# Ten of sixteen weight loads issued from ScalarE's queue in place of SyncE's, in an attention and mixture-of-experts kernel

## The chip, the cores and the metric

The kernel runs on one core of a Trainium2 chip. The metric is the device time of one execution in microseconds; the kernel before took 539.23 us (median of three runs, 539.05 to 540.62). The names of the engines are those of the profile: PE (matmul, with PEld for its weight loads), DVE (vector engine), ACT (scalar engine), POOL, and SP, which only issues transfers. ACT can issue transfers too, on a queue of its own.

## The reference

Attention that keeps the 32 largest scores of each row, followed by a dense mixture of four experts:

```python
scores = scale * np.matmul(q, k.transpose(0, 1, 3, 2))      # 2 x 8 heads, 576 x 576, head dim 64
kth = np.partition(scores, -top_k, axis=-1)[..., -top_k:-top_k + 1]      # top_k = 32
scores = np.where(scores >= kth, scores, -1000000000.0)
attn = np.exp(scores - np.max(scores, axis=-1, keepdims=True))
attn = attn / (np.sum(attn, axis=-1, keepdims=True) + 1e-09)
x = np.matmul(attn, v)                                       # -> 1152 x 512
...
p = domain_probs / (domain_probs.sum(-1, keepdims=True) + 1e-09)
for e in range(E):                                           # 4 experts, 512 -> 1024 -> 512
    h = np.maximum(x @ w1[e], 0.0)
    out += p[:, e:e + 1] * (h @ w2[e])
```

## The kernel before

The 1152 rows are cut into ten tiles: for each of two batches four of 128 rows and one of 64. The first tile worked on is the 64-row tile of batch 0. A tile is cut into units, one for each head (four units of two heads for a 64-row tile); they are numbered u = 0, 1, 2, ... through the whole program. For one unit PE computes the scores (`emit_qk`, L643), DVE finds the 32 largest by four rounds of MAX8 and three of MATCH_REPLACE8 (`topk_op`, L656 to L660), ACT takes the exponential (`emit_exp`, L700), DVE or ACT and POOL apply the mask (L707 to L717), ACT and POOL split the result into two fp16 halves (`emit_a`, L725 to L729), a DMA transposes it (`emit_at`, L735, issued by SP), and PE multiplies it by v (`emit_av`, L765). When all heads of a tile are done, the experts run on it: `m1` (L882 to L884), `h_hi` and `h_lo`, `m2` (L929), `evac`.

The expert weights are eight matrices, named by (e, j): expert e, j = 0 for w1 and j = 1 for w2. Each is loaded in two halves of 1 MB (`load_w`, L342; halves a = 0 and a = 2), so there are sixteen loads. Each matrix then goes through four steps. `w_gram` (L498) is 32 matmuls on PE that run over the raw matrix: the first 16 read the half a = 0, the last 16 the half a = 2. `w_diag` (L504 on DVE, L507 on PE) and `w_total` (L280, L282 on DVE) make a scale out of that. `w_raw` (L527, ACT) scales the raw matrix, and `w_split` (L533 on ACT, L536 on POOL) cuts it into fp16 halves, the form that the experts use. The order in which the matrices are taken is (0,0), (1,0), (0,1), (1,1), (2,0), (3,0), (2,1), (3,1). The two matrices of expert 3 take the place of a scratch area that the first tile uses, so their loads wait until that is free.

Every step is a function registered with `at`. A table `ISSUE` gives each step its place in one global order, and each engine executes its instructions strictly in that order: an instruction that waits holds up all that stands behind it on its engine. The transfers of SP and ACT, in the global order, use eight completion semaphores in turn, so an issue also waits until the eighth transfer before it has landed.

In the global order the ten loads that the change touches stand at these places on ACT's side: both halves of (1,0) between two L1086 instructions at about 21.7 us of the trace; the first half of (0,1) between an L533 and an L700 at 31.1; its second half between an L1101 and an L573 at 34.1; both halves of (1,1) between an L700 and an L527 at 36.2; both halves of (2,0) between an L533 and an L700 at 56.4; half a = 2 of (2,1) between an L533 and an L700 at 62.0; half a = 0 of (2,1) between an L533 and the first L893 at 66.3. On PE the `w_gram` of (2,0) stands between the scores of unit 7 and those of unit 8; behind it follow the first `m1` and the scores of units 9 and 10.

Of the kernel before, what the change touches and what calls it, by code (L numbers as in the profile page):

```python
# [229 lines left out]
def attn_moe_kernel(tc, q, k, v, probs, w1, w2, out):  # L230
    nc = tc.nc
    PE, ACT, DVE, POOL, SP = nc.tensor, nc.scalar, nc.vector, nc.gpsimd, nc.sync
# [29 lines left out]
    def at(place, fn, *args):  # L262

        i = len(known)
        known.append(fn.__name__)
        heapq.heappush(events, (ISSUE[i][0] if ISSUE else place, i, 0, fn, args))
# [20 lines left out]
    with tc.manual_schedule(engines={getattr(mybir.EngineType, x) for x in MANUAL}):  # L287
# [202 lines left out]
        def w_scale(e, j, place):  # L490
            st = {}

            def w_gram():
                st["g"] = g = bank(ps_m1, "m1")
                hi16 = wt[e, j].rearrange("p c f -> p (c f)").bitcast(BF16)
                hi16 = hi16.rearrange("p (n t) -> p n t", t=2)[:, :, 1]
                for c in range(32):
                    PE.matmul(g[:, 0:128], lhsT=hi16[:, c * 128:(c + 1) * 128], rhs=hi16[:, c * 128:(c + 1) * 128],  # L498
                              start=(c == 0), stop=(c == 31))

            def w_diag():
                g = st["g"]
                dg = stp.tile([128, 1], F32, tag="gd", name="gd")
                DVE.scalar_tensor_tensor(g[:, 0:128], g[:, 0:128], 1.0, ident, op0=OP.mult, op1=OP.mult, accum_out=dg)  # L504
                yield
                st["pt"] = g[:, 256:257]
                PE.matmul(st["pt"], lhsT=ones, rhs=dg, start=True, stop=True)  # L507

            def w_total():
                s = ws[:, e, j:j + 1]  # L510
                wscale[e, j] = s
                yield from pow2(st, st["pt"], C_W2 if j else C_W1, 1, "w", dst=s, inv=iw[:, e, j:j + 1])
                if (e, j) == (WORDER[-1], 1):
                    yield 1
                    DVE.tensor_tensor(iwp, iw[:, :, 0], iw[:, :, 1], op=OP.mult)
                    yield 1
                    iwb = iwp.rearrange("p (g e) -> p g e", g=1).to_broadcast([128, 5, E])
                    DVE.tensor_tensor(pniw[:, 0:5], pn[:, 0:5], iwb, op=OP.mult)

            at(place, w_gram)  # L520
            at(place + P["diag"], w_diag)
            at(place + P["wtot"], w_total)
# [604 lines left out]
        swap = 10 * last_of[tiles[0]] + P["av_first"] + 1  # L1127
# [70 lines left out]
        for m, (e, j) in enumerate(worder):  # L1198
            for a in (0, 2):
                n = 4 * m + a  # L1200
                x = P["w_load"] + P["w_load_pace"] * (n - P["w_early"])
                if n < P["w_early"]:
                    x = P["w_first"] if n < 3 else P["w_second"]
                at(max(x, swap + 0.1) if e == 3 else x, load_w, SP, e, j, a, a + 2)
            g = P["gram"][m]
            w_scale(e, j, g)
            g = max(P["split"][m], g + P["diag"], raw_used.get((e, j), 0) + 0.1)
            for i in range(2):
                at(g + 2 * P["wsplit_pace"] * i - 0.1, w_raw, e, j, i)
            for i in range(4):  # L1210
                at(g + P["wsplit_pace"] * i, w_split, e, j, i, W_MODE[4 * m + i])

        while events:
            place, i, n, f, args = heapq.heappop(events)
# [38 lines left out]
```

## Time and profile before

| | |
|---|---|
| median of three runs | 539.23 us |
| the profiled execution | 540.16 us, of which the span of the trace is 538.4 us |
| PE busy, whole span | 505.1 us (94%) |
| DVE busy | 433.7 us (81%) |
| ACT busy | 365.0 us (68%) |
| POOL busy | 361.4 us (67%) |

The span falls into two parts. Up to about 118 us the weights are loaded and prepared and the first tiles pass through attention; after that PE works nearly without a break. Busy shares of the whole span mix the two parts, so engines are read by stretches. "Idle before" behind an instruction tells how long its engine stood still before it and what released it. The DMA-issuing instructions of SP and ACT appear as SPq and ACTq.

### The profile page before, as it was taken

Reading aid. Unit: us, or ns where it says so; the run is one execution under the profiler, and the core shown is the slowest. Engines: PE = TensorE matmul, PEld = TensorE weight load, DVE = VectorE, ACT = ScalarE, POOL = GpSimd, SP = SyncE. Lnnn points to the kernel's source line nnn. Section 1 sums busy time; section 2 is a strip of 40 time slices with the busy share of each in tenths; the row PEclk is TensorE's granted clock in tenths of the full one; section 3 lists DMA queues with packets and bytes.
Section 4 is the critical chain, followed back from the end, with each engine's and each line's share of the span. In section 5 each row is a group of like instructions: output and inputs, shape, how many; then the busy total and the mean of one; then the engine's idle time right before and its main releaser. Section 6 shows DMA issues by size and latency. Waiting matters only on the chain.

```text
span 538.4 us, 16332 instructions
## 1 busy us (share of the span) xinstructions
PE 505.1 (94%) x6738; PEld 384.6 (71%) x6738; DVE 433.7 (81%) x969; ACT 365.0 (68%) x602; POOL 361.4 (67%) x397
## 2 busy tenths in 40 slices
PE   7887758699999999999999999999999999999996
PEld 5666644586778677777777678677777778667766
DVE  3999997999999999999999989999999686610101
ACT  2999997998777777897768666764656635442121
POOL 0499997999877677978967866574665754253211
PEclk9997798799999999999999999999999999999999
DMA  8999998552474277574553642452423322214001
GB/s 218 311 255 331 265 280 170 104 90 47 99 144 75 65 111 128 94 139 93 122 113 88 110 70 66 83 89 45 76 52 62 71 45 47 43 24 65 12 2 32
DMA packets 142779, 58.37 MB, mean 108 GB/s; under 512 B 130096, under 2 KB 134448, under 8 KB 142704
## 3 DMA queue, kind: packets, MB, share of 16 engines
q1 hardware_dynamic: 139280, 54.50, 49.9%
q10 hardware_dynamic: 3424, 2.82, 1.7%
q8 instruction: 53, 0.87, 0.7%
q14 instruction: 22, 0.18, 0.1%
HBM read 25.45 MB, written 2.36 MB: 52 GB/s over the span
## 4 chain that ended last, share of the span: by engine, by line
PE 78%; DVE 14%; DMA 2%; ACT 2%; SPq 2%; issue 1%; POOL 0%; DVEq 0%
PE m L929 34%; PE m L882 11%; PE m L883 11%; PE m L884 11%; DVE m L656 6%; PE av L765 5%; PE ps L643 5%; DVE w L660 3%; DVE w L658 2%; DVE w L707 2%; DMA at<-a 2%; DMA pn<-in_moe_domain_probs_dram 1%; ACT w L533 1%; ACT w L527 1%; PE m L940 1%
## 5 line engine op out<-in xcount | busy, mean ns | idle before, releaser
L884 PE MATMUL m<-xt,w 128*128 128x128 f16 (+1 forms) x1280 | 199.8, 215 | 0.1
L929 PE MATMUL m<-w,h 128*128 128x512 f16 (+1 forms) x912 | 191.4, 383 | 0.0
L882 PE MATMUL m<-xt,w 128*128 128x128 f16 (+1 forms) x1120 | 178.9, 215 | 0.0
L883 PE MATMUL m<-xt,w 128*128 128x128 f16 (+1 forms) x1120 | 178.8, 215 | 0.0
L656 DVE MAX8 m<-w 128x8 f32<-128x576 f32 x216 | 161.6, 754 | 3.2
L929 PEld LDWEIGHTS <-h 128*128 128x128 f16 (+1 forms) x912 | 81.6, 101 | 88.4 <-issue 2.2
L884 PEld LDWEIGHTS <-w 128*128 128x128 f16 x1280 | 124.0, 99 | 0.2 <-POOL w L536 0.2
L882 PEld LDWEIGHTS <-w 128*128 128x128 f16 x1120 | 108.8, 99 | 2.6 <-issue 1.0
L907 POOL TENSOR_TENSOR h<-hf,h 128x512 f16<-128x512 f32 x59 | 68.4, 1160 | 62.6 <-ACT hf L900 62.2
L883 PEld LDWEIGHTS <-w 128*128 128x128 f16 x1120 | 108.5, 99 | 1.6
L660 DVE MATCH_REPLACE8 w<-m,w 128x576 f32<-128x576 f32 x144 | 106.9, 742 | 0.0
L727 POOL TENSOR_TENSOR a<-w,a 128x512 f16<-128x512 f32 x68 | 78.9, 1161 | 32.9 <-ACT a L725 17.9
L700 ACT ACTIVATE w<-ps,nb,es 128x576 f32<-128x576 f32 x68 | 56.3, 829 | 52.3 <-DVE m L656 46.1
L717 POOL TENSOR_TENSOR w<-w,d 128x576 f32<-128x576 f32 x48 | 61.4, 1282 | 27.6 <-ACT d L714 27.5
L893 ACT ACTIVATE h<-m 128x512 f16<-128x512 f32 x72 | 42.4, 593 | 53.5 <-PE m L884 35.9
L656 DVE MAX8 m<-ps 128x8 f32<-128x576 f32 x72 | 54.3, 755 | 15.2 <-PE ps L599 8.2
L725 ACT ACTIVATE a<-w 128x576 f16<-128x576 f32 x68 | 45.9, 679 | 13.2 <-POOL w L717 12.0
L658 DVE MATCH_REPLACE8 w<-m,ps 128x576 f32<-128x576 f32 x72 | 53.8, 747 | 0.0
L643 PE MATMUL ps<-kt,qa 128*128 128x288 f16 x128 | 34.9, 292 | 10.9 <-DVE w L707 10.0
L765 PEld LDWEIGHTS <-at 128*128 128x128 f16 (+1 forms) x1008 | 36.9, 101 | 9.1 <-DMA at<-a 3.5
L765 PE MATMUL av<-vt,at 128*128 128x65 f16 (+1 forms) x1008 | 39.4, 196 | 3.2 <-DMA at<-a 3.2
L900 ACT ACTIVATE hf<-m 128x512 f32<-128x512 f32 x59 | 34.9, 591 | 7.5 <-POOL h L907 6.0
(166 smaller groups left out, 759.1 us busy)
## 6 DMA issues: line engine op xcount, KB each, us to landing
w<-in_moe_w_dram SPq DMA_DIRECT2D x16, 1024.0 KB, 8.1
qraw<-in_q_dram SPq DMA_DIRECT2D x8, 256.0 KB, 3.4
qb<-qa SPq DMA_DIRECT2D x16, 128.0 KB, 2.6
out_dram<-o ACTq DMA_DIRECT2D x8, 256.0 KB, 2.2
at<-a SPq DMA_TRANSPOSE x68, 3.3
vraw<-in_v_dram SPq DMA_DIRECT2D x2, 512.0 KB, 7.4
nraw<-in_v_dram SPq DMA_DIRECT2D x4, 256.0 KB, 2.9
kraw<-in_k_dram SPq DMA_DIRECT2D x4, 256.0 KB, 2.9
```

The costliest lines, as they stand in the source:

```text
L643: PE.matmul(ps[:, 0:288], lhsT=src[:, x, :], rhs=kt[x].rearrange("p c n -> p (c n)")[:, ks], start=(j == 0), stop=(j == 1))
L656: DVE.max(m, s_t[u] if r == 0 else w_t[u])
L658: DVE.match_replace(rows2(w_t[u]), m, s_t[u], NEG)
L660: DVE.match_replace(w_t[u], m, w_t[u], NEG)
L717: POOL.tensor_tensor(w, w, g, op=OP.mult)
L727: POOL.tensor_tensor(a[:, 640:1152], w[:, 0:512], a[:, 0:512], op=OP.subtract)
L765: PE.matmul(o, lhsT=att[:, blk, ps], rhs=r, start=(i == 0), stop=(i == len(seq) - 1))
L882: PE.matmul(o, lhsT=HI[e, 0, c][:, fc], rhs=xs(0, c), start=(c == 0), stop=False)
L883: PE.matmul(o, lhsT=HI[e, 0, c][:, fc], rhs=xs(1, c), start=False, stop=False)
L884: PE.matmul(o, lhsT=LO[e, 0, c][:, fc], rhs=xs(0, c), start=False, stop=(c == 3))
L907: POOL.tensor_tensor(h[:, 1], hf, h[:, 0], op=OP.subtract)
L929: PE.matmul(y[z * 64:z * 64 + M, :], lhsT=h_t[es, qd][:, p // 2, h0:h0 + M], rhs=w, start=(fc == 0 and p == 0), stop=(fc == 7 and p == 2))
```

## The change

One line of the loop that places the weight loads. Every load was issued by SP; now the two halves of (0,0) and the four halves of expert 3's matrices stay with SP, and all others go to ACT. That is ten loads by the condition in the code (a short description of the change speaks of eight). The places in the global order are the same. The data that each load moves, the tile that it fills and the steps that read it are unchanged.

```diff
--- before.py
+++ after.py
@@ -1201,7 +1201,7 @@
                 x = P["w_load"] + P["w_load_pace"] * (n - P["w_early"])
                 if n < P["w_early"]:
                     x = P["w_first"] if n < 3 else P["w_second"]
-                at(max(x, swap + 0.1) if e == 3 else x, load_w, SP, e, j, a, a + 2)
+                at(max(x, swap + 0.1) if e == 3 else x, load_w, SP if e == 3 or n < 4 else ACT, e, j, a, a + 2)
             g = P["gram"][m]
             w_scale(e, j, g)
             g = max(P["split"][m], g + P["diag"], raw_used.get((e, j), 0) + 0.1)
```

Here `n` is 4 times the place of the matrix in the order above plus the half `a`, so `n < 4` is the matrix (0,0).

## Rows read from the trace of the kernel before

**Rows 1.** Stretches: from, to, length, busy us of PE, PEld, DVE, ACT, POOL; clock.
```profile
10.00:118.00 108.00, 81.92 (x1242) 67.61 (x1241) 103.59 (x269) 100.11 (x126) 92.09 (x68) 0.89 0.97 232
20.00:56.00 36.00, 27.02 (x357) 22.24 (x355) 35.83 (x94) 35.74 (x45) 31.42 (x22) 0.91 1.16 288
118.00:538.00 420.00, 416.14 (x5459) 312.25 (x5455) 329.29 (x698) 262.27 (x472) 268.30 (x316) 1.00 0.40 75
```

**Rows 2.** Timeline of SP: start, duration us, line, transfer, count.
```profile
31.70 4.84 SPq L342 DMA_DIRECT2D w<-in_moe_w_dram  x3
...
43.77 0.58 SPq L342 DMA_DIRECT2D w<-in_moe_w_dram  x1
...
48.82 1.75 SPq L342 DMA_DIRECT2D w<-in_moe_w_dram  x1
...
63.04 3.04 SPq L342 DMA_DIRECT2D w<-in_moe_w_dram  x3
```

**Rows 3.** Timeline of ACT, at the places named above.
```profile
35.42 0.74 ACT L700 ACTIVATE w<-ps,nb 128x576 f32<-128x576 f32 x1
...
55.46 1.05 ACT L533 ACTIVATE w<-w 128x1024 f16<-128x1024 f32 x1
56.41 0.82 ACT L700 ACTIVATE w<-ps,nb,es 128x576 f32<-128x576 f32 x1
...
66.32 0.58 ACT L893 ACTIVATE h<-m 128x512 f16<-128x512 f32 x1
```

**Rows 4.** Timeline of ACT around one store that ACT issues (ACTq).
```profile
428.64 0.58 ACT L893 ACTIVATE h<-m 128x512 f16<-128x512 f32 x1
428.66 0.34 ACTq L983 DMA_DIRECT2D out_dram<-o  x1
429.12 0.59 ACT L900 ACTIVATE hf<-m 128x512 f32<-128x512 f32 x1
```

**Rows 5.** Weight loads by window: issue ns min/median/max and starts; us to landing.
```profile
L342 SPq DMA_DIRECT2D w<-in_moe_w_dram x2: 583/1167/1751, 43.8 to 48.8; - x2
DMA to landing us min/median/max: 6.7/7.4/8.2
...
L342 SPq DMA_DIRECT2D w<-in_moe_w_dram x3: 601/725/1623, 63.0 to 64.5; - x3
DMA to landing us min/median/max: 8.3/10.2/12.0
...
L342 SPq DMA_DIRECT2D w<-in_moe_w_dram x14: 367/594/2176, 16.7 to 83.3; - x14
```

**Rows 6.** Waits of SP: who waited, for whom, us in total, times, longest.
```profile
SPq L328 <- DMA w<-in_moe_w_dram: 0.4, 1, 0.4
```

**Rows 7.** Timeline of PE.
```profile
52.31 1.08 PE L498 MATMUL m<-w 128*128 128x128 bf16 x16
57.02 1.89 PE L498 MATMUL m<-w 128*128 128x128 bf16 x16 [3.64 <-DMA w<-in_moe_w_dram]
...
70.85 0.30 PE L643 MATMUL ps<-kt,qa 128*128 128x288 f16 x1 [2.60 <-DVE w L707]
...
76.31 0.28 PE L643 MATMUL ps<-kt,qb 128*128 128x288 f16 x1
79.81 0.76 PE L765 MATMUL av<-vt,at 128*128 128x65 f16 x14 [3.21 <-DMA at<-a]
...
85.33 0.36 PE L507 MATMUL m<-gd,ones 128*128 128x1 f32 x2
```

**Rows 8.** Timeline of DVE.
```profile
60.17 0.75 DVE L656 MAX8 m<-ps 128x8 f32<-128x576 f32 x1
...
81.38 0.79 DVE L707 SCALAR_TENSOR_TENSOR w<-ps,m,w 128x576 f32<-128x576 f32 x1
85.72 0.16 DVE L280 TENSOR_SCALAR wpt<-m 128x1 int32<-128x1 int32 x1 [3.55 <-PE m L507]
```

**Rows 9.** The chain of work that ended last, in order of time.
```profile
71.40 8.36 DMA at<-a
```

## The prediction

> **What bounds the kernel now.** I read the stretches first. From 10 to 118 us DVE is busy 103.59 of 108.00 us, ACT 100.11, PE only 81.92; from 118 us to the end PE is busy 416.14 of 420.00 [rows 1]. So the second part is a fixed amount of PE work in a fixed order: whatever delays PE at 118 us delays the end by as much, and nothing there gives it back. The first part is DVE's, and DVE stands still there for 4.4 us in all. That is the most that any change of the loads can win. Of this, 3.55 us is one wait, at 85.72, for a small PE matmul [rows 8]. PE came late to that matmul because it had stood still for 3.21 us until 79.81 for a transposed tile [rows 7], whose DMA took 8.36 us from 71.40 on [rows 9].
>
> The next view is the timeline of PE at the weight loads. The `w_gram` of (2,0) reads its first half at 52.31, then PE waits 3.64 us for the second half and goes on at 57.02 [rows 7]. That half was issued by SP at 48.82 [rows 2] and landed 8.2 us later [rows 5]. So this load is already the one that PE waits for; its first half was issued at 43.77 [rows 2]. In PE's order the scores of unit 8 stand behind it, and DVE takes them up at 60.17 [rows 8], 3.15 us after PE went on.
>
> **The change: no work is removed.** All sixteen loads remain, with the same bytes. Ten issues leave SP's stream and enter ACT's. What changes is when they are issued and who is held up.
>
> **When they are issued.** SP ran ahead of ACT wherever its own waits allowed. On ACT a load comes up only when all ACT work before it has been started. The two halves of (2,0) stand behind the L533 that starts at 55.46, ahead of the L700 at 56.41 [rows 3]. So they go from 43.77 and 48.82 to about 56 us. For the other eight the shift is small: (1,1) from 32 to 34 us [rows 2] to about 36 [rows 3]; the rest of the early ones move by 0 to 5 us, the halves of (2,1) by 3 to 6, and the `w_gram` of (2,1) stands in PE's order behind that of (2,0) and much else, so these have time.
>
> **What an issue costs ACT.** ACT has no slack from 20 to 56 us: 35.74 of 36.00 us busy [rows 1]. A store issued by ACT shows how an issue lies beside the work: it begins at 428.66, 0.02 us after the L893 began at 428.64, and the next instruction follows at 429.12 as if it were not there [rows 4]. So the sequencer issues while the instruction before it still executes, and an issue is free as far as that instruction covers it. A weight load's issue took 0.594 us in the median on SP [rows 5]. Single ones, each behind an instruction of 1.05 us or more, cost nothing. A pair takes 1.19 us and has 0.74 us of cover behind the L700 at 35.42 [rows 3]: about 0.45 us lost, and as much at the pair of (1,0). So ACT comes to its 55.46 place about 1.0 us late. The bounds: nothing lost at all, and six issues of the longest kind, 2.176 us each [rows 5], 13.1 us, less 0.74 us of cover at each of the four places, 10.1 us. I take 1.0 because ACT's own row shows covered issues; it is nearer to the median than to a case with many transfers queued.
>
> **What a wait on ACT costs.** A load also waits for the eighth transfer before it; SP once waited 0.4 us in this way [rows 6]. For (2,1) that transfer is now a half of (2,0), which lands at about 63 us or later, while ACT reaches the place at about 63. That may stop ACT for 0 to 2 us, with the exponential of unit 7 queued behind it and DVE's mask of unit 7 waiting for that. It is covered: ACT next needs the first `m1` at its L893 (66.32 before [rows 3]), which stands on PE behind the late `w_gram`, so ACT has some 7 us in hand there.
>
> **Landing of (2,0).** First half issued at 55.46 + 1.0 = 56.5, second at 57.1. Bounds for the second: 6.7 us (the quickest of a pair) and 12.0 us (the last of three in a row) [rows 5]. With one load ahead it is 8.2, with two ahead 10.2 [rows 5]; here one is ahead on the same queue and a load of (3,0) is issued by SP about 58 us on the other, so I take the middle, 9.2: it lands at 66.3. PE's second half of `w_gram` goes from 57.02 to 66.3, **+9.3 us**, and DVE's unit 8 with it.
>
> **What is given back.** DVE's work from 60.17 to the end of the L707 at 81.38 + 0.79 = 82.17 is unbroken [rows 8], so it now ends at 91.5. PE waits for DVE before the scores of unit 10 (2.60 us at 70.85 [rows 7]), so these move to 80.2; the PE work from there to the scores that end at 76.6 is 5.7 us, so the product that began at 79.81 begins at 85.9. Its transposed tile is by then long there: it was in place at 79.76 [rows 9], and even 3 us later is before 85.9. So the 3.21 us wait is gone and PE is 6.1 us late. The small matmul of L507 needs a DVE step that is 9.3 us late, which I estimate to add 0.4. The matmul at 85.33 then comes 6.5 us late and DVE's 85.72 becomes 92.2; DVE is free at 91.5, so its 3.55 us wait shrinks to 0.7. **+6.5 us** stays. From there to 118 us DVE has hardly a gap, and after that PE has none.
>
> The Trainium skill, "DMA: Bandwidth & Descriptors", section "Queues, rings and completion order", says that each DMA engine takes turns between the queues that have work. By that, a transpose on SP's queue would no longer stand behind a weight load on ACT's, and the 8.36 us transfer [rows 9] would be shorter. It leaves the sum as it is, since the wait for that transfer is gone anyway; it matters for the second rival.
>
> **The sum.** The profiled execution took 540.16 us, so its counterpart is 546.7. It lies 0.9 us above the median 539.23, and on the median the forecast is **545.7 us** (+1.2%).
>
> **The rivals.** (1) *Issues stop ACT for their whole time.* For it: ACT is full, and three issues in a row took 4.84 us on SP [rows 2]. Against it: the store on ACT [rows 4]. With the 10.1 us bound, the halves of (2,0) are issued at 65.6 and 66.2 and the second lands at 66.2 + 10.2 = 76.4, +19.4 on PE, less 3.4 given back: about +16, 555.2 us. Chance 0.12.
>
> (2) *Faster: the transposes are freed.* Place: the product at 79.81 and DVE's wait at 85.72. Price: 3.4 us, 535.8 us. It decides only if the second half of (2,0) lands less than 3.4 us later than before, by 60.4. From an issue at 57.1 that is 3.3 us, against 6.7 as the quickest row [rows 5]. It needs ACT to issue earlier than its order of starts tells. Chance 0.07.
>
> (3) *Same: only the queue changes.* If ACT's sequencer ran several instructions ahead, the loads of (2,0) would be issued early enough to land by about 60, the lateness would be eaten by PE's 3.21 us wait, and the time would stay at 539.2. The row of the store shows one instruction of lead, no more [rows 4]. Chance 0.08. The Trainium skill, same page, section "Issuing engines are not separate DMA queues", says that issuing from several engines only saves the sequencer's time to issue. By that rule alone the time would stay, since SP is no bound here; that an issue moves behind another engine's work is not in it.
>
> **How the numbers follow.** Forecast 0.73, the rivals 0.12, 0.07 and 0.08. The forecast's own range: at the low end no loss on ACT and a landing 6.7 us after 56.1, so 62.8, +5.8 - 3.2 = +2.6, 541.8 us. At the high end each of six issues costs ACT its 0.594 us (3.6 us) and the landing takes 12.0: 55.46 + 3.6 + 0.6 + 12.0 = 71.7, +14.7 - 3.4 = +11.3, 550.5 us. Extended a little toward the rivals: 541 to 552. A measurement of this kernel can tell about 0.3% (1.6 us) from no change. Slower by more than that: 0.85; within it: 0.08; faster: 0.07.
>
> **What would show it.** In the new profile the loads of (2,0) stand on ACT's queue at 56 to 58 us; PE waits for the weights at L498 for some 13 us in place of 3.64; DVE, unbroken before, stands still about 9 us just before the scores of unit 8; the waits at 79.81 and 85.72 shrink; every later row is some 6 to 7 us late, and PE's busy time after that is the same. ACT shows gaps of about half a microsecond at the two pairs. I am wrong if the loads are issued well before ACT's L533 at 55.46, if they land in less than 6 us, or if ACT loses more than 4 us before 56 us.

## The result and the profile after

The changed kernel took 546.0 us (median of four runs, 544.53 to 548.37) beside 539.14 us for the kernel before (four runs, 538.35 to 540.62): a ratio of 1.0128, with a 95% interval of 1.0082 to 1.0175, or 6.9 us. The forecast was 545.7. Here and below a time is the median of the executions in the faster of two states that the chip shows. The profiled execution took 547.07 us with a span of 545.2 us, against 540.16 and 538.4 before.

The stretches of the kernel after come first (columns as in [rows 1]); the last row is the second part, moved by the lateness.

```profile
10.00:118.00 108.00, 79.39 (x1131) 64.44 (x1129) 96.46 (x253) 93.33 (x116) 85.06 (x63) 0.81 0.90 229
20.00:56.00 36.00, 27.43 (x349) 22.20 (x346) 31.76 (x84) 30.87 (x39) 26.47 (x18) 0.86 0.87 231
124.00:545.00 421.00, 416.96 (x5471) 313.24 (x5468) 330.05 (x699) 263.03 (x473) 268.88 (x317) 1.00 0.40 75
```

From 124 us on PE is busy 416.96 of 421.00 us, as it was from 118 us on [rows 1]: nothing is lost or won there. All of it is in the first part, where DVE is busy 96.46 of 108.00 us in place of 103.59, and already 4.1 us less from 20 to 56 us. The granted clock of the first part is lower too, 0.81 against 0.89, with PE standing still more; it counts only as far as DVE waits for PE, which it does at the third place below.

Where DVE stood still is in its timeline (start, length, line, operation; in brackets the idle time before it and what ended it). Between the first mask of a unit (L707) and the sixteenth the waits over 0.2 us are these three; before there was one, the 3.55 us at 85.72 [rows 8].

```profile
39.95 0.16 DVE L280 TENSOR_SCALAR wpt<-m 128x1 int32<-128x1 int32 x1 [3.84 <-PE m L507]
...
66.03 0.15 DVE L280 TENSOR_SCALAR qpt<-qss 128x1 int32<-128x1 int32 x1 [2.64 <-ACT qhl L373]
...
87.22 0.30 DVE L504 SCALAR_TENSOR_TENSOR m<-m,ident 128x128 f32<-128x128 f32 x1 [2.12 <-PE m L498]
```

With the smaller gaps that the timeline shows (over 0.15 us) DVE stands still 9.19 us there, and 3.75 before. The difference is 5.4 us. The first mask itself started 0.73 us later (18.86 against 18.13), before ACT issues any load; its start differs by more than that between executions, as the last section tells, so this part is not put down to the change.

**First place, 30 to 40 us.** First two rows of the kernel before, with the time that q's transpose took to land, then the queues and engines of the kernel after:

```profile
20.46 1.36 SPq L394 DMA_TRANSPOSE qa<-qhl  x1
27.03 1.28 SPq L1093 DMA_TRANSPOSE kt<-khl  x1
...
qa<-qhl SPq DMA_TRANSPOSE x1, 5.3
```

```profile
20.66 1.36 SPq L394 DMA_TRANSPOSE qa<-qhl  x1
31.42 12.40 SPq L1093 DMA_TRANSPOSE kt<-khl  x7
...
qa<-qhl SPq DMA_TRANSPOSE x1, 9.5
...
21.16 0.47 ACTq L342 DMA_DIRECT2D w<-in_moe_w_dram  x1
...
33.60 1.35 ACT L1101 ACTIVATE vraw<-vraw,vps 128x1280 f32<-128x1280 f32 x1
39.14 0.42 ACTq L342 DMA_DIRECT2D w<-in_moe_w_dram  x1
39.61 0.60 ACT L573 ACTIVATE at<-m 128x512 f32<-128x512 f32 x1 [4.66 <-DMA kt<-khl]
...
38.58 0.40 PE L643 MATMUL ps<-kt,qa 128*128 128x288 f16 x1 [3.47 <-DMA kt<-khl]
```

Two things happen at once. (A) The transpose of q, issued at 20.66, took 9.5 us to land (the row that ends in 9.5: us from issue to landing); before, the same transpose, issued at 20.46, took 5.3 and landed at 25.7. Half a microsecond behind it, and again half a microsecond later, ACT had issued the two loads of (1,0). SP's next step needs q, so the first k transpose went out at 31.42 in place of 27.03. It took 7.1 us in place of 3.5, landing 0.5 us behind the load that ACT had issued at 30.63, and PE waited 3.47 us for it. The small matmul for which DVE waits 3.84 us stands in PE's order behind the scores that wait for k. (B) ACT was done with its L1101 at 34.95 and then stood still 4.66 us until a k transpose of SP had landed. The L573 that carries this idle time does not read k. What stands ahead of it in ACT's order is the load at 39.14. In the trace that load has the same completion semaphore as the k transpose that SP issued at 33.60, which landed at 39.1: the load goes out as soon as it has landed. The next load goes out at 39.75, as the k transpose issued at 34.94 has landed (39.7). In this trace B lies beside A, and DVE's 3.84 us are A's.

**Second place, 56 to 66 us.** The first two rows are again of the kernel before:

```profile
52.93 1.19 SPq L817 DMA_TRANSPOSE xt<-xhl  x1
...
xt<-xhl SPq DMA_TRANSPOSE x1, 4.5
```

```profile
56.58 0.37 ACTq L342 DMA_DIRECT2D w<-in_moe_w_dram  x1
...
60.59 1.05 ACT L533 ACTIVATE w<-w 128x1024 f16<-128x1024 f32 x1
...
65.28 0.63 ACT L373 ACTIVATE qhl<-qraw 128x512 bf16<-128x512 f32 x1 [2.92 <-DMA xt<-xhl]
...
58.10 1.23 SPq L817 DMA_TRANSPOSE xt<-xhl  x1
...
xt<-xhl SPq DMA_TRANSPOSE x1, 7.1
...
61.60 1.89 PE L498 MATMUL m<-w 128*128 128x128 bf16 x16 [4.12 <-DMA w<-in_moe_w_dram]
64.61 1.89 PE L498 MATMUL m<-w 128*128 128x128 bf16 x16 [1.12 <-DMA w<-in_moe_w_dram]
```

(C) The loads of (2,0) went out at 56.58 and 56.99. In ACT's order they stand behind the L533 that starts at 60.59, so ACT issued the first 4.0 us ahead of that instruction's start; five instructions of ACT, this L533 the last, begin between 56.60 and 60.59. They landed after 5.0 and 7.6 us, and PE takes up their halves at 61.60 and 64.61. DVE's 2.64 us is not that chain: it waits for ACT's L373, and ACT waits 2.92 us for the transpose of xt, which took 7.1 us (before, issued at 52.93, 4.5 us). Before, too, xt landed 0.5 us behind the second load of (2,0), which stood ahead of it on SP's own queue; now it lands 0.6 us behind the one that ACT issued. Then that load had been issued 4.1 us ahead of xt, now 1.1 us.

**Third place, 80 to 88 us.** The first two rows are the `w_gram` of (3,0) and of (2,1) in the kernel before, the others are of the kernel after:

```profile
71.50 2.00 PE L498 MATMUL m<-w 128*128 128x128 bf16 x32
73.90 2.01 PE L498 MATMUL m<-w 128*128 128x128 bf16 x32
```

```profile
68.65 2.35 SPq L342 DMA_DIRECT2D w<-in_moe_w_dram  x2
...
80.34 3.57 PE L498 MATMUL m<-w 128*128 128x128 bf16 x32 [1.12 <-POOL a L727]
84.49 2.70 PE L498 MATMUL m<-w 128*128 128x128 bf16 x32
87.83 0.62 PE L765 MATMUL av<-vt,at 128*128 128x65 f16 x14 [0.16 <-DMA at<-a]
```

(D) DVE's step on the `w_gram` of (2,1) (87.22 above) waits 2.12 us, because PE is late. It isn't the landing of (2,1): its halves, issued by ACT at 66.39 and 72.11, took 9.7 and 11.6 us, the second landed at 83.7, and PE, busy without a gap from 80.34 on, comes to them only at 84.49. PE is late at the `w_gram` before, that of (3,0). One half of (3,0), which SP issued at 68.65, took 11.4 us and landed at 80.1, where before it had taken 8.33 and landed in time; PE waits 1.12 us and starts at 80.34. (The row puts the end of this wait down to POOL, whose instruction ends 0.1 us after the landing; in two of the experiments the same wait is longer and the row names the load.) And PE is then slower: the granted clock is 1.00 (2.4 GHz) until 79.2 us and 0.50 (1.2 GHz) from there to 86.0; when it fell PE had stood still for 2.60 us, worked for 0.65 us and come to this wait. Before, the same 2.60 us were followed by work without a gap, and the clock stayed at 1.00. The two `w_gram` take 3.57 and 2.70 us in place of 2.00 and 2.01, so the low clock costs more here (2.3 us) than the wait. That the wait brought it about isn't shown: with only (2,0) on ACT, below, the clock was at 0.52 behind 2.60 us of standing still alone. The give-back is there too: PE's wait for the transposed tile is 0.16 us in place of 3.21 [rows 7], and DVE's 3.55 us wait [rows 8] is gone.

### The profile page after: what moved, and what is told of

Its sections match the earlier page's. It is cut to its first block, busy times and chain, and to the rows that moved or that the text cites. A ratio compares the mean times of both kernels' runs of the same rounds, so it can differ in the third digit from the quotient of the medians.

```text
span 545.2 us, 16330 instructions
## 1 busy us (share of the span) xinstructions
PE 508.1 (93%) x6738; PEld 387.3 (71%) x6738; DVE 434.6 (80%) x969; ACT 365.2 (67%) x602; POOL 360.9 (66%) x397
## 3 DMA queue, kind: packets, MB, share of 16 engines
HBM read 25.45 MB, written 2.36 MB: 51 GB/s over the span
## 4 chain that ended last, share of the span: by engine, by line
PE 77%; ACT 4%; DVE 2%; DMA 2%; issue 2%; POOL 1%; POOLq 0%
PE m L929 33%; PE m L882 11%; PE m L883 11%; PE m L884 11%; PE av L765 5%; PE ps L643 5%; DMA at<-a 2%; ACT w L533 1%; ACT w L527 1%; DVE m L656 1%; ACT a L725 1%; PE m L940 1%; PE av L940 0%; PE ps L639 0%; DVE w L660 0%
## 5 line engine op out<-in xcount | busy, mean ns | idle before, releaser
L700 ACT ACTIVATE w<-ps,nb,es 128x576 f32<-128x576 f32 x68 | 56.3, 828 | 50.6 <-DVE m L656 45.3
L765 PE MATMUL av<-vt,at 128*128 128x65 f16 (+1 forms) x1008 | 39.7, 196 | 0.2 <-DMA at<-a 0.2
```

The lines of the kernel that those rows point to most:

```text
L700: ACT.activation(rows2(w_t[u]), s_t[u], AF.Exp, bias=nb, scale=es)
L765: PE.matmul(o, lhsT=att[:, blk, ps], rhs=r, start=(i == 0), stop=(i == len(seq) - 1))
```

## The experiments

Two theories stood against each other. The forecast's: only the lateness of (2,0) costs anything, less the give-back. The other, out of the trace after: the cost is a sum over places A, B, C and D, less the give-back of 3.5 us. Most experiments give only some matrices to ACT, by the condition in line 1204; the base is the kernel before.

**Only (1,0) on ACT.**

```diff
-  at(..., load_w, SP, e, j, a, a + 2)
+  at(..., load_w, ACT if (e, j) == (1, 0) else SP, e, j, a, a + 2)
```

> Only the two loads of (1,0) go to ACT's queue, the other fourteen stay with SP. Theory F (the forecast: all that counts is the late issue of (2,0)): at most 0.5 us on ACT, so 539 to 540 us. Theory K (in the profile after, q's transpose takes 9.5 us beside the loads of (1,0) where it took 5.3, SP waits for it before the transposes of k, and DVE stands still about 4 us at 36 to 40 us): the same 4 us stand here alone, qa lands after some 9 us, about 543 us.

Measured: 540.03 us, ratio 1.0023 [0.9992, 1.0054], no difference. The transpose of q, issued at 21.38, landed after 6.0 us, at 27.4; SP sent the first k transpose at 28.70, 1.7 us later than before, and DVE has no wait near 38 us. The second theory's 4 us for A aren't there with (1,0) alone.

**Only (2,0) on ACT**, condition `(e, j) == (2, 0)`.

> Only the two loads of (2,0) go to ACT's queue. Theory F: issued at about 56 us, PE's gram of (2,0) some 9 us late, 3.4 us given back: 545 to 546 us. Theory K (in the profile after, ACT issued these loads 4 us ahead of the start of the instruction that they stand behind): issued at about 52 us, landed by 59 or 60, PE 2 to 3 us late, which the waits at 79.81 and 85.72 take up: 539 to 541 us.

Measured: 541.51 us, 1.0051 [1.0015, 1.0088]: slower by about 2.5 us, less than half of what the forecast put on this part. ACT and DVE of this kernel:

```profile
52.84 0.42 ACTq L342 DMA_DIRECT2D w<-in_moe_w_dram  x1
61.63 0.63 ACT L373 ACTIVATE qhl<-qraw 128x512 bf16<-128x512 f32 x1 [3.01 <-DMA xt<-xhl]
...
62.38 0.15 DVE L280 TENSOR_SCALAR qpt<-qss 128x1 int32<-128x1 int32 x1 [2.62 <-ACT qhl L373]
```

The wait C is there by itself, in nearly the size that it has in the changed kernel. In the profiled execution (541.03 us) it is paid back: the wait at 85.72 shrinks to 0.39 us. Where the other executions lose their 2.5 us isn't shown.

**All but (1,0)**, condition `(e, j) in ((0, 1), (1, 1), (2, 0), (2, 1))`.

> As the changed kernel, but the loads of (1,0) stay with SP: eight loads on ACT. Theory F: as the changed kernel, 545 to 546 us. Theory K: the 4 us at 36 to 40 us are gone, and the later waits, which were 2.6 and 2.2 us less 3.5 given back, are left: 540 to 542 us.

Measured: 545.43 us, 1.0109 [1.0072, 1.0146]. The transpose of q took 4.9 us and landed at 24.8, so A is gone, and yet the kernel is hardly quicker than the changed one. DVE's waits, and PE's at D:

```profile
38.79 0.82 DVE L707 SCALAR_TENSOR_TENSOR w<-ps,m,w 128x576 f32<-128x576 f32 x1 [1.92 <-ACT w L700]
...
63.31 0.15 DVE L280 TENSOR_SCALAR qpt<-qss 128x1 int32<-128x1 int32 x1 [2.87 <-ACT qhl L373]
...
78.88 3.43 PE L498 MATMUL m<-w 128*128 128x128 bf16 x32 [1.91 <-DMA w<-in_moe_w_dram]
...
84.62 0.30 DVE L504 SCALAR_TENSOR_TENSOR m<-m,ident 128x128 f32<-128x128 f32 x1 [2.24 <-PE m L498]
```

B comes up from behind A, here with ACT standing still 2.90 us until a weight load has landed; C and D stay. At D the row of PE names the load that it waits for, and that is the half of (3,0) on SP's queue (issued at 65.78, 12.9 us to land).

**All but (2,0)**, condition `(e, j) in ((1, 0), (0, 1), (1, 1), (2, 1))`.

> As the changed kernel, but the loads of (2,0) stay with SP: eight loads on ACT. Theory F: the cause is gone, 539 to 541 us. Theory K: the 4 us at 36 to 40 us stay, about 543 us.

Measured: 550.27 us, 1.0189 [1.0138, 1.0239]. Without the one part on which the forecast rested, the kernel is not quicker; this is what breaks the forecast's mechanism. It is slower than both theories said.

```profile
39.90 0.60 ACT L573 ACTIVATE at<-m 128x512 f32<-128x512 f32 x1 [5.77 <-DMA kt<-khl]
...
40.29 0.16 DVE L280 TENSOR_SCALAR wpt<-m 128x1 int32<-128x1 int32 x1 [4.78 <-PE m L507]
...
87.35 0.30 DVE L504 SCALAR_TENSOR_TENSOR m<-m,ident 128x128 f32<-128x128 f32 x1 [3.22 <-PE m L498]
```

The transpose of q took 9.7 us. A and B stand at 40 us, D at 87 (PE waits 2.70 us for the half of (3,0)), and no C: the transpose of xt, with no load under way, landed after 2.5 us.

**Only (0,1) and (1,1)**, condition `(e, j) in ((0, 1), (1, 1))`, and the same kernel a second time.

> Only the four loads of (0,1) and (1,1) go to ACT's queue. Theory F (only (2,0) counts): 539 to 540 us. Theory K, enlarged by the runs so far: ACT stops at the second half of (0,1), because the semaphore that this load takes belongs to a transpose of k or a load that has not landed (4.7 us in the changed kernel, 2.9 with (1,0) on SP); DVE loses some 2 us near 38 us while q's transpose stays at 4 to 5 us. What the waits at 79.81 and 85.72 then give back decides the end: 538 to 541 us.

> The kernel that gives only (0,1) and (1,1) to ACT once more, for a second trace: its timed runs (546 to 548) lay 3 to 5 us above the execution that was profiled (542.9). If the wait at L700 near 50 us varies from run to run, this trace shows it longer than 4.84 us or a second wait beside it, and 546 to 548; if it is a matter of the profiled run alone, 542 to 544 again with one wait of 4.8.

Measured: 547.12 us, 1.0128 [1.0058, 1.0198] for the first; 548.15 us, 1.0153 [1.0057, 1.0249] for the second. Four of the ten loads cost as much as all ten. ACT's and DVE's rows of the first trace, whose execution took 542.92 us:

```profile
37.24 4.89 ACTq L342 DMA_DIRECT2D w<-in_moe_w_dram  x2
42.57 2.00 ACT L527 ACTIVATE w<-w,ws 128x2048 f32<-128x2048 f32 x1 [5.71 <-DVE w L658]
...
50.53 0.82 DVE L707 SCALAR_TENSOR_TENSOR w<-ps,m,w 128x576 f32<-128x576 f32 x1 [4.84 <-ACT w L700]
```

ACT stands still 5.71 us where its only pending business is the second of two loads; the DVE step named as releaser had long been done. That load, issued at 41.76, shares its semaphore with the k transpose issued at 36.00, which landed at 41.7. DVE waits 4.84 us behind it, and the wait at 85.72 is gone. The second trace, of an execution of 547.21 us:

```profile
50.18 0.82 DVE L707 SCALAR_TENSOR_TENSOR w<-ps,m,w 128x576 f32<-128x576 f32 x1 [5.41 <-ACT w L700]
...
92.76 0.16 DVE L280 TENSOR_SCALAR wpt<-m 128x1 int32<-128x1 int32 x1 [3.75 <-PE m L507]
...
86.77 0.62 PE L765 MATMUL av<-vt,at 128*128 128x65 f16 x14 [2.58 <-DMA at<-a]
```

Here the give-back failed. The transposed tiles of a landed after 5.5 us in the median of 66 to 96 us, against 3.6 in the first trace, and the wait for one is back. DVE's 3.75 us wait is most of the 4.3 us between the two executions of one and the same program, so what the kernel before can give back isn't certain.

**Only (2,1)**, condition `(e, j) == (2, 1)`.

> Only the two loads of (2,1) go to ACT's queue. Theory F: their gram has time, 539 us. Theory K (three profiles with (2,1) on ACT show DVE standing still for 2.1 to 3.2 us near 85 us behind PE's gram of (2,1)): the second issued half lands after PE has come to it, 1 to 3 us lost there, of which the wait at 85.72 gives back most: 538 to 541 us.

Measured: 539.81 us, 1.003 [0.999, 1.007], no difference. D appears, and the wait at 85.72 vanishes for it:

```profile
74.47 3.57 PE L498 MATMUL m<-w 128*128 128x128 bf16 x32 [2.20 <-POOL h L907]
...
81.20 0.30 DVE L504 SCALAR_TENSOR_TENSOR m<-m,ident 128x128 f32<-128x128 f32 x1 [3.03 <-PE m L498]
```

The size is as expected, the path isn't: both halves of (2,1) have landed by 77.7, and PE comes to them at 78.62. PE had waited 2.20 us for the half of (3,0), which SP issued at 62.70, 0.34 us sooner than before, and which took 11.6 us in place of 8.33; then it worked at a granted clock of 0.50. No other load is on ACT here, so moving (2,1) is enough to delay (3,0) on SP.

**The give-back tried alone:** all loads on SP, the first half of (3,1) later in the order, so that the transpose at 71.40 [rows 9] doesn't stand behind it.

```diff
- ]
+ ]; ISSUE[1575] = (341.5,)          # was 316
```

> The kernel before, all loads on SP; only the first half of (3,1) is issued three transposes later in SP's order (behind the transposes of units 6 and 4 and of q), where it is still in time for its gram at 89 us. It tests what the 8.36 us transpose before PE's wait at 79.81 is made of. If it stands behind the weight loads in the queue, it lands 2 to 3 us sooner, the wait of DVE at 85.72 shrinks from 3.55 to about 1 us: 536 to 537.5 us. If not, 539 us.

Measured: 540.78 us, 1.002 [0.999, 1.0051]. The transpose landed after 4.0 us in place of 8.36, as expected if it had stood behind the load. PE's wait at 79.81 is gone, and the next tile is late instead: its transpose, issued 1.4 us behind the moved load, took 6.8 us, and DVE waits 2.36 us behind it.

```profile
85.14 0.95 PE L765 MATMUL av<-vt,at 128*128 128x65 f16 x14 [2.77 <-DMA at<-a]
```

**(2,0) alone, at an earlier place of ACT's order.**

```diff
- ]
+ ]; ISSUE[1542] = (188.3,); ISSUE[1543] = (188.6,)    # were 223, 231
-  at(..., load_w, SP, e, j, a, a + 2)
+  at(..., load_w, ACT if (e, j) == (2, 0) else SP, e, j, a, a + 2)
```

> As the run with only (2,0) on ACT, but its two loads stand earlier in ACT's order, between two w_split instructions that ACT starts at about 46 us, so they are issued at 43 to 46 us, as SP did in the kernel before. Same queue, same bytes, another place. If the place is the cause (issued at 52.8 us, the loads ran beside the transpose of the first tile's x, for which ACT waits before it squares the next q, 2.6 us for DVE), the wait of 2.6 us and most of PE's 3.6 us at the second half are gone: 538 to 539 us. If the second queue as such is the cause, they stay, and the time stays at 541 us.

Measured: 539.0 us, 1.0017 [0.9978, 1.0057], no difference from before. With the loads at 46.73, more than 7 us ahead of the transpose of xt at 54.22, that transpose took 4.8 us and C is gone:

```profile
46.73 0.94 ACTq L342 DMA_DIRECT2D w<-in_moe_w_dram  x2
...
59.12 0.63 ACT L373 ACTIVATE qhl<-qraw 128x512 bf16<-128x512 f32 x1 [0.60 <-DMA xt<-xhl]
```

Its profiled execution, with 0.38 us of DVE standing still, took 538.25 us; single runs went from 537.2 to 542.3, so it can't be called quicker than the kernel before. The loads are still on ACT's queue: what made C was their place, 1.0 to 1.5 us ahead of xt, and not the second queue as such.

**(0,1) and (1,1) at earlier places.**

```diff
- ]
+ ]; ISSUE[1520] = (97.5,); ISSUE[1521] = (103.5,); ISSUE[1531] = (111.5,); ISSUE[1532] = (114.5,)
                                                       # were 108, 130, 138, 142
-  at(..., load_w, SP, e, j, a, a + 2)
+  at(..., load_w, ACT if (e, j) in ((0, 1), (1, 1)) else SP, e, j, a, a + 2)
```

> Only the loads of (0,1) and (1,1) go to ACT, as in the run that moved these four alone (547.1), but in ACT's order they stand 3 to 4 us sooner, ahead of the exponentials that they stood behind. Theory B (ACT stands still at a load that needs the completion semaphore of a k transpose issued by SP, 4.7 to 5.8 us, and DVE behind it 4.84 us): where the place of the load in the order moves, another transfer is the eighth before it; if B is the cause, DVE's wait of 4.84 us for L700 near 50 us is gone or under 1 us and the time is 538 to 541. Rival, any two queues at once slow the k transposes whatever the place: the wait stays above 3.5 us and the time is 544 to 548. Forecast's theory (only the lateness of (2,0) counts): 539 to 540, and it did not foresee the 547.1.

Measured: 548.97 us (three executions), 1.0237 [1.0139, 1.0335], no quicker than without the earlier places. Theory B's number was not met: the earlier place was no remedy. DVE's wait for L700 stayed above the rival's 3.5 us, and the time lies above its range. But the rows show B at its clearest:

```profile
34.40 0.20 ACT L668 ACTIVATE nb<-m 128x1 f32<-128x1 f32 x1 [2.71 <-DMA qb<-qa]
34.51 1.04 ACT L533 ACTIVATE w<-w 128x1024 f16<-128x1024 f32 x1
43.61 0.38 ACTq L342 DMA_DIRECT2D w<-in_moe_w_dram  x1
44.19 1.36 ACT L1101 ACTIVATE vraw<-vraw,vps 128x1280 f32<-128x1280 f32 x1 [8.64 <-DMA kt<-khl]
...
47.44 0.82 DVE L707 SCALAR_TENSOR_TENSOR w<-ps,m,w 128x576 f32<-128x576 f32 x1 [8.54 <-ACT w L700]
```

ACT ends its L533 at 35.55, and nothing of ACT runs until the load goes out at 43.61. An L668, which reads only DVE's maxima, waits for a copy of q, and an L1101 for a transpose of k: both stand behind a load. This last load of (1,1) waits for the semaphore that one of the k transposes raises. At its old place that was the fifth k transpose (36.00 to 41.7); at the earlier one it is the fourth, as theory B supposed, but that one, issued at 33.30, took 10.3 us and landed at 43.6, 0.5 us behind the load that ACT had issued at 33.91. So ACT comes to the load sooner and waits longer, for a transpose that lands only behind ACT's own load.

**Three matrices at earlier places**: the two edits above together, condition `(e, j) in ((0, 1), (1, 1), (2, 0))`.

> The loads of (0,1), (1,1) and (2,0) go to ACT, all at earlier places of ACT's order (those of the two runs that moved them by groups); (1,0) and (2,1) stay with SP. If the cost of the change is a matter of place (where a load stands among ACT's work and between SP's transposes) and not of the queue, 537 to 540, DVE waiting less than 2 us in all between 30 and 90 us. If two queues at once cost by themselves, 543 to 547.

Measured: 545.85 us (seven executions), 1.0116 [1.0074, 1.0159]. Its profiled execution took 540.85 us, with one wait of DVE (2.21 us at 40.52, for L700); the timed ones took 2.8 us longer and more. No trace shows where those lose it, so this run doesn't decide between its two theories: the trace speaks for the first, the median for the second.

**(1,0) sooner**, so that its loads are under way when q's transpose is issued.

```diff
- ]
+ ]; ISSUE[1509] = (51.5,); ISSUE[1510] = (51.6,)      # were 62, 65
-  at(..., load_w, SP, e, j, a, a + 2)
+  at(..., load_w, ACT if (e, j) == (1, 0) else SP, e, j, a, a + 2)
```

> Only the loads of (1,0) go to ACT, two places sooner, so that they are under way when SP issues the transpose of q at about 20.7 us. Theory A (that transpose takes 9.5 us in place of 5.3 because two loads of the other queue run beside it; the k transposes behind it on SP are then late): q lands 9 to 10 us after its issue, PE waits 3 us or more for k near 38 us, DVE 3 to 4 us, 542 to 544. Rival A2 (the transpose is slow only where SP's own queue is emptied of all the loads, so that SP issues it earlier than the loads land): q in 5 to 7 us, no wait of DVE near 38 us, 539 to 540.5.

Measured: 539.52 us, 1.0012 [0.9975, 1.005], no difference. In the trace it lies between the two theories: q, issued at 21.63, took 7.6 us and landed at 29.2, k went out at 30.53, DVE waited 2.24 us, and the wait at 85.72 vanished for it. So (1,0) alone does bring A about, in a smaller size, and it costs nothing as long as the reserve at 85.72 is unspent.

```profile
42.66 0.77 DVE L656 MAX8 m<-ps 128x8 f32<-128x576 f32 x1 [2.24 <-PE ps L643]
```

**All traces in one sum.** If the end is set by when DVE gets through the first part, then the time of a profiled execution is the start of the first L707, plus what DVE stands still between the first L707 and the sixteenth (gaps over 0.15 us), plus a constant:

| kernel | profiled us | first L707 | DVE idle | the rest |
|---|---|---|---|---|
| before | 540.16 | 18.13 | 3.75 | 518.3 |
| after | 547.07 | 18.86 | 9.19 | 519.0 |
| only (1,0) | 540.96 | 19.39 | 2.80 | 518.8 |
| only (2,0) | 541.03 | 19.41 | 3.21 | 518.4 |
| all but (1,0) | 545.62 | 17.58 | 8.86 | 519.2 |
| all but (2,0) | 546.85 | 17.23 | 10.48 | 519.1 |
| (0,1), (1,1) | 542.92 | 18.51 | 6.01 | 518.4 |
| the same again | 547.21 | 17.89 | 10.74 | 518.6 |
| only (2,1) | 540.46 | 18.31 | 3.79 | 518.4 |
| (3,1) later | 540.99 | 19.20 | 3.42 | 518.4 |
| (2,0) earlier | 538.25 | 19.40 | 0.38 | 518.5 |
| (0,1), (1,1) earlier | 547.36 | 17.98 | 10.70 | 518.7 |
| three earlier | 540.85 | 19.46 | 2.74 | 518.7 |
| (1,0) sooner | 540.36 | 19.31 | 2.44 | 518.6 |

The rest stays within 0.9 us over fourteen executions, while DVE's idle time goes from 0.4 to 10.7 us. From the start of the sixteenth L707 to the end of the span it is 420.6 to 420.8 us in all fourteen: nothing behind that point wins or loses. That is the account of the change between the two profiled executions: DVE's standing still, 5.4 us more, and 1.5 us of start and rest, make their 6.9 us.

## Why the prediction was right, and where it was not

**What bounds the kernel: right.** DVE bounds the first part and PE the second, and a lateness at 118 us is carried to the end; the table above is that statement over all the runs.

**The total: right by two errors that cancel, which is luck.** The forecast had +9.3 us at one place and +6.5 after the give-back. The trace after has 3.84, 2.64 and 2.12 us at three places, less 3.55, which is 5.1; the later start and small gaps make up the rest. Of the three, only the second is a place that the forecast named, and it came about by another path. All three signs that the prediction gave for being wrong are in the trace: the loads of (2,0) went out 4.0 us ahead of the L533 that they stand behind, the first landed in 5.0 us, and ACT stood still 4.66 us before 56 us.

**When (2,0) is issued: the time right, the reason wrong.** Forecast 56.5 and 57.1, measured 56.58 and 56.99. But ACT was 5.1 us late by then (the L533 at 60.59 against 55.46 [rows 3]), not 1.0 us, and its sequencer ran 4 us ahead. Neither was foreseen. I had read one instruction of lead out of the store [rows 4]; that row sets a lower bound on the lead, and I took it for the lead. The third rival had this mechanism right. In the run with only (2,0) on ACT the loads went out at 52.84, 3.7 us ahead of my 56.5, and with nothing else moved the cost was 2.5 us.

**Landing of (2,0) and its +9.3 us: the term that was mis-sized.** 5.0 and 7.6 us to land, not 9.2 for the second; PE's waits for the two halves are 4.12 and 1.12 us, where I wanted some 13, and DVE lost 2.64 us there, by another path: xt's transpose, 7.1 us beside the loads, and ACT's L373 behind it. That chain isn't in the prediction. Nor did a load of (3,0) run beside these, as the forecast had it: SP issued the first one at 66.11, not at 58.

**What an issue costs ACT: nothing in the trace after.** Its issues of 0.37 to 0.56 us lie beside ACT's work, the pairs too; the gaps of half a microsecond that I wanted at the pairs aren't there. (In the kernel with three matrices earlier one issue took 1.24 us, and ACT stood still 0.40 us behind it.) The first rival, an issue that stops ACT for its whole time, falls with them.

**The wait on ACT: the mechanism right, place and size wrong.** I named the wait for an earlier transfer, but put it at (2,1), with 0 to 2 us, covered. It came at the second half of (0,1), with 4.66 us, and in the other runs with 2.6 to 8.6 us (in one of them, 2.90 us, for a weight load): among the loads at 31 to 43 us the earlier transfers are mostly SP's k transposes. At (2,1), too, it was a k transpose (landed at 65.9, load out at 66.39) and a load of q, not a half of (2,0). I had looked only for weight loads as the earlier transfers.

**Loads "for which the shift is small": wrong.** (0,1) and (1,1) alone cost as much as the whole change. In the trace after, their four loads went out 2.3, 7.4, 7.4 and 6.1 us later than before, not 0 to 5; and what I did not cost is that on SP a load takes its turn among the transposes, and on ACT it runs beside them, and holds up ACT's own work when it has to wait. Of (2,1) it was right that it had time; what I left out is that its loads, issued later and on ACT, delay the half of (3,0) on SP for which PE waits (D).

**The queues side by side.** The Trainium skill, "DMA: Bandwidth & Descriptors", section "Queues, rings and completion order", says that each DMA engine takes turns between queues; by that I had the transposes on SP's queue quicker. In the runs no transpose gains by standing on another queue than the loads. The transpose of xt took 7.1 to 7.2 us in the three kernels in which ACT issued the loads of (2,0) 1.0 to 1.5 us ahead of it, and 2.5 to 5.1 us in the eleven other traces. What counts there is how much of a load is still under way, not whose queue it is on: xt landed 0.5 to 0.6 us behind the last load ahead of it in those three, and 0.5 us behind in the three (the kernel before, only (2,1), (1,0) sooner) in which SP had issued that load, 3.6 to 4.1 us ahead. The transpose of q landed at 27.4 to 30.1 us in the four kernels with (1,0) on ACT, and at 24.5 to 26.6 us in the ten others, although SP issues a 1 MB load 1.4 us behind it there. Whether the loads of (1,0) delay q by their queue or by coming nearer to it (0.0 to 1.2 us behind, or ahead) was not separated. The rule may hold for each DMA engine; that a transpose gains by it is not what these rows show. The page's section "Issuing engines are not separate DMA queues" says that several issuers only save the time to issue. No run here shows anything else saved, and the moved order costs 1.3%.

**The give-back: right in the trace after, and not certain.** 3.21 became 0.16 on PE, 3.55 became 0 on DVE. It is also why single parts cost little: (1,0), (2,0) and (2,1) alone each make a wait of up to 3 us, and in their traces the wait at 85.72 shrinks or vanishes for it; only (2,0) alone is slower beyond its interval, by about 2.5 us. The 3.55 us can be spent once, so the parts don't add: the first is nearly free and the next ones cost in full.

**What stays open.** How much the loads of (1,0) delay q: it landed at 27.4 with their issues 0.8 and 1.2 us behind its own, at 30.1 with 0.5 and 1.0 us, at 29.3 with 0.0 and 0.5 us, at 29.2 with both ahead, each in one trace; what sets the size wasn't found. And what the timed runs of the kernel with three matrices earlier, and of the one with all but (2,0), lose beyond their traces (2.8 us and more); a slow transpose of a, as in the second trace of (0,1) and (1,1), is a candidate that was not seen in them.

## What to carry to other kernels

A transfer moved to another engine's queue changes more than its issue time: list, for each moved issue, which transfer it must wait for under the shared completion semaphores, and what compute stands behind it on its new engine; a wait that cost nothing on an engine that only issues costs in full on one that computes. Look also at which small transfers (transposes here), and which loads that are needed soon, will now be issued just behind it, on whatever queue. A wait late in the stage that bounds the kernel is a reserve that swallows the first few microseconds of any loss ahead of it, so parts tested one by one can each look free.

## What the runs showed of the hardware that was not expected

- ACT's sequencer issued a load 4.0 us ahead of the start of the instruction before it (56.58 against 60.59), with five instructions not yet begun, not one; so too with (2,0) alone (52.84 against 56.86).
- Small transposes by DMA are slowed by 1 MB loads that the other queue got at nearly the same time, as they are by one ahead on their own queue: xt 7.1 to 7.2 us against 2.5 to 5.1, q 9.5 and 9.7 us (6.0 and 7.6 where (1,0) alone was moved) against 3.3 to 6.3.
- The same program gave 542.92 and 547.21 us in two traced executions, by how fast transposes of 66 to 96 us landed (3.6 or 5.5 us in the median).
- The first L707 started between 17.23 and 19.46 us in fourteen executions, 19.20 in a program that is the same as the kernel before (18.13) up to 63 us: 1.1 us of the spread is there without any change.
- Behind a wait of 0.8 to 2.7 us for the half of (3,0), in five traces, PE's granted clock was 0.50 to 0.60 in place of 1.00, and the `w_gram` took 3.0 to 3.6 us in place of 2.00.
